# Gated attention and hash-routed experts on one core: the small token blocks of the experts, cut in halves and turned round on TensorE

## The chip, the cores and the metric

The kernel runs on one NeuronCore of one Trainium2 chip. The metric is device time in microseconds (us) of one execution; the smaller the better. A profiled execution comes with it: a span, busy times of the engines, and a trace. In the profile PE is TensorE's matrix multiplication, PEld its loading of the stationary operand, DVE is VectorE, ACT ScalarE, POOL GpSimd, and SP the engine that issues most DMAs. All data is float32. The profile writes two records for every float32 matmul, and two loads of the stationary operand.

## The reference

```python
# attention: u, v (8, 2496, 256), z (8, 2496, 64)
scores = (1 / S) * np.matmul(z, z.transpose(0, 2, 1))
attn = np.maximum(scores, 0.0) ** 2
x = (u * np.matmul(attn, v)).reshape(B * S, D)          # 19968 tokens of 256
# experts: w1 (8, 256, 1024), w2 (8, 1024, 256)
expert_idx = token_ids * np.int64(2654435761) % np.int64(8)
for e in range(8):
    xe = x[expert_idx == e]
    out[expert_idx == e] = np.maximum(xe @ w1[e], 0.0) @ w2[e]
```

Each of the 19968 tokens goes through the one expert that its id selects. With the fixed inputs of the reference, the eight experts get 2483, 2535, 2394, 2497, 2468, 2469, 2634 and 2488 tokens.

## The kernel before

**Attention.** The 2496 tokens of a batch are 20 tiles of 128 (the last has 64 rows). Queries are taken in five groups of four tiles, so there are 40 groups. For each group TensorE makes `s_ps` (scores, one matmul of up to 512 columns per key tile; the contraction is only 64 deep, and neighbouring tiles sit on the lower and the upper 64 partitions of `zT`, so that they use the two halves of the array's rows), ScalarE takes ReLU and square into `a`, and TensorE sums `acc`, which is v times `a` (L350; L358 for the 64-row tile). Scores are symmetric: VectorE transposes 32x32 blocks of `a` into tiles `m` ("mirrors") for later groups instead of computing them again (`turns_of`, L257). Some pairs of groups (`CARRIED`) are turned as a whole into `stage` (L261) and moved to their partitions by DMA, with one of the four moves a ScalarE copy (L270). How many transposes are put in at each step is planned by `turn_scores` with a budget of VectorE time, and `turn_now` puts in what is left when a tile is about to be read or its room reused. `between()` runs at each step and hands out small work: the routing arithmetic in `places()` for the first `SORT` steps, then the writing of each token's slot (`enter`), and of gated rows into `x_rows` in DRAM, in slot order (`place_x`).

**First batch.** `load_z` brings z by DMA on SP, VectorE copies one tile, TensorE transposes pairs of tiles into `z_ps` (`turn_z`), and VectorE and ScalarE copy the halves into `zT`. Six matmuls on zeros (`warm`) run before.

**Experts.** Slots are grouped by expert. 32 *wholes* have 512 tokens each (`NW`), and what remains of each expert is cut into *parts* of 128 tokens. At most 35 parts can be needed (`NP`); 33 of them (`NU`) are run always, and an `If` covers the rest, which these inputs don't need: they fill 32. The order is written out by hand: whole, part, whole, part, ..., with one part more at the end: 65 blocks.

For each block `load_x` fetches its tokens, `load_w` fetches w1 and w2 of its expert (1 MB each), `turn_x` transposes 32x32 blocks of the tokens on VectorE, `ups` multiplies by w1, and ReLU goes in turn to ScalarE and VectorE (L776, L778). `down` multiplies by w2 for 128 tokens at a time (L784); ScalarE copies the result, and GpSimd scatters the rows to `out` (L796). In `ups` w1 is the stationary operand and the tokens move:

```python
for i in range(m):                       # m = 1 in a whole, 4 in a part
    for c in range(DP):                  # DP = 2
        nc.tensor.matmul(ps[:, ts(i, n)], w1[j][:, c, ts(k * m + i, P)], xT[j][:, :, c, :], ...)
```

So a whole has 16 matmuls with 512 moving columns, a part 16 with 128. Both give `hT`, activations with features on partitions, which `down` takes as the stationary operand, while w2 moves 256 columns: 8 matmuls for each 128 tokens.

`run` is a software pipeline. In step i it issues the load of the tokens of block i + 2, then the banks of `ups` of block i with the `down`s of block i - 1 put between them (a part's `down` comes after two banks of the whole that follows; a whole's four `down`s come after the second bank of the part), then the weights of block i + 2. There are three pairs of weight buffers, which are mirrors that attention no longer needs. PSUM has six banks for `h_ps`, `s_ps`, `z_ps` (one pool, `mm_ps`) and two for `o_ps` and `acc`.

Of the kernel before, what the change touches and what calls it, by code (L numbers as in the profile page):

```python
# [24 lines left out]
def kernel(  # L25
# [33 lines left out]

    BLK = 512  # L60
    NW = -(-(N - E * (BLK - 1)) // BLK)
    NP = (N - NW * BLK + E * (P - 1)) // P
    NU = (N - NW * BLK) // P + E // 2 + 1
    NB = NW + NP
    CLEAR = T // 2
    NS = NW * BLK // P + NP
# [61 lines left out]
    def load_z(b):  # L128
        if b == 0:

            zn[b] = npool.tile([P, T + 1, K], F32, name="zn")
            tiles_io(zf, b, range(T), zn[b][:, 1:, :], False, nc.sync, twice=True)
            nc.vector.tensor_copy(zn[b][:, 0, :], zn[b][:, T, :])
            return
        zn[b] = npool.tile([P, T, NQ, Q], F32, name="zn")
        rows = zf[ds(b * S, S), :]
        for q in range(NQ):
            cols = ts(q % 2, Q)
            o = zn[b][ts(q, Q)]
            for t, m in ((slice(0, TM), rows[0:SM, cols].rearrange("(j i t) k -> i t j k", i=Q, t=TM)),  # L140
                         (TM, rows[SM:S, cols].rearrange("(j i) k -> i j k", i=Q))):
                if t == TM:
                    for h in range(2):
                        nc.sync.dma_start(o[:, TM, ds(h * R // Q, R // Q), :], m)
                else:
                    nc.sync.dma_start(o[:, t], m)
# [10 lines left out]
    def turn_z(b, g):  # L157
        if g == 0:
            zT[b] = zpool.tile([P, T * P], F32, name="zT")
        o = zT[b][:, ts(g, G * P)]  # L160
        if b:
            nc.vector.transpose(o, zn[b][:, ts(g, G)].rearrange("p t j k -> p (t j k)"))
            return


        ps = mm_ps.tile([P, G * P], F32, name="z_ps", tag="mm")
        for i, t in enumerate(group(g)):
            nc.tensor.transpose(ps[:, ts(i, P)], zn[b][:, t:t + 2].rearrange("p t k -> p (t k)"), ident[:])
        nc.vector.tensor_copy(o[K:P], ps[K:P, :])  # L169
        i = 0 if g else 1  # L170
        nc.scalar.copy(zT[b][0:K, ds((g * G + i - 1) * P, (G - i) * P)], ps[0:K, i * P:])  # L171
        return ps
# [74 lines left out]
    def turns_of(b, a, g):  # L247
# [10 lines left out]
        def carry(c):  # L258
            m = room()
            stage = spool.tile([P, G * G * Q], F32, name="stage")  # L260
            nc.vector.transpose(stage[:].rearrange("p (n q) -> p n q", q=Q), x[:, :, ts(c, Q)])  # L261
            for r in range(NQ):

                n = tiles_of(g, r)
                o = m[ts(c, Q), 0:n, r].rearrange("p i s q -> p i (s q)")
                y = stage[ts(r, Q), 0:n * G * Q].rearrange("p (i x) -> p i x", i=n)
                if r != c:
                    nc.sync.dma_start(o, y)
                else:
                    to_fetch.append((i + 3, key, lambda o=o, y=y: nc.scalar.copy(o, y)))  # L270
# [33 lines left out]
    def turn_scores(steps):  # L304
# [5 lines left out]
        carried = i % 2  # L310
# [14 lines left out]
    def fetch(due):  # L325
        for e in [e for e in to_fetch if due(e)]:
            to_fetch.remove(e)
            e[2]()

    def turn_now(key):  # L330
        for e in [e for e in to_turn if e[0] == key]:
            turn(e)
        fetch(lambda e: e[1] == key)
# [27 lines left out]
    def gate(b, g, h, acc):  # L361
# [26 lines left out]
        to_fetch.append((i + 3, None, rows_of_x))  # L388
# [15 lines left out]
    def clear_x(k):  # L404
        c = NW * BLK // P + k * -(-NP // CLEAR)
        n = min(NS - c, -(-NP // CLEAR))
# [10 lines left out]
    def places():  # L417

        with tc.tile_pool(name="route", bufs=1) as route:
# [3 lines left out]
            iota_b = route.tile([1, NP], F32)  # L423
            nc.gpsimd.iota(iota_b[:], pattern=[[1, NP]], base=0, channel_multiplier=0,
# [17 lines left out]
            mask = room[:, E * C:E * C + E * C // 2].bitcast(BF16).rearrange("p (e c) -> p e c", e=E)  # L442

# [18 lines left out]
            for e in range(0, E, H):  # L462
# [17 lines left out]
            per_e = route.tile([P, 12, E], F32)  # L480
            first, count, whole, upto_w, before_w, rest, parts, upto_p, thr, start, jump, late = (
                per_e[:, k, :] for k in range(12))
# [7 lines left out]
            int_e = route.tile([P, E], I32)  # L490
            nc.vector.tensor_copy(int_e[:], count)
# [11 lines left out]
            nc.vector.tensor_scalar(int_e[:], rest, float(P - 1), None, op0=OP.add)  # L503
            nc.vector.tensor_scalar(int_e[:], int_e[:], P.bit_length() - 1, None, op0=OP.logical_shift_right)
            yield
            nc.vector.tensor_copy(parts, int_e[:])
            nc.vector.tensor_tensor_scan(upto_p, ones[:, 0:E], parts, 0.0, op0=OP.mult, op1=OP.add)
            yield

# [7 lines left out]
            yield  # L517

            def wide(a):
                return a.unsqueeze(2).to_broadcast([P, E, C])  # L520

            nc.vector.tensor_tensor(total, rank, wide(thr), op=OP.is_ge)
            yield
            nc.gpsimd.tensor_mul(total, total, wide(jump))
            yield
# [3 lines left out]
            ahead = upto[:, :, C - G - 1]  # L529
# [7 lines left out]
            nc.gpsimd.tensor_add(rank, rank, total)  # L537
            least = route.tile([P, 1], F32)
            nc.vector.tensor_reduce(least[:], late, axis=AX.X, op=OP.min)
            yield  # L540
# [4 lines left out]
            nc.vector.tensor_copy(used[:], upto_p[0:1, E - 1:E])  # L545
# [4 lines left out]

            over = route.tile([1, NB, E], F32)
            for a, n, ends in ((0, NW, upto_w), (NW, NP, upto_p)):
                nc.vector.tensor_tensor(
                    over[:, a:a + n], ends[0:1].unsqueeze(1).to_broadcast([1, n, E]),
                    iota_b[:, 0:n].unsqueeze(2).to_broadcast([1, n, E]), op=OP.is_le)
            yield
            eb = route.tile([1, NB], F32)
            nc.vector.tensor_reduce(eb[:], over[:], axis=AX.X, op=OP.add)
            yield
            nc.vector.tensor_scalar(eb_i[:], eb[:], float(E - 1), None, op0=OP.min)  # L560
            for _ in range(5):
                yield
# [37 lines left out]
    WARM = 6  # L600
    order = tc.manual_schedule()
    order.__enter__()


# [4 lines left out]
    load_z(0)  # L609
# [3 lines left out]
    z_ps = [turn_z(0, g) for g in range(NG)]  # L613
    nc.scalar.copy(zT[0][0:K, ts(TM, P)], z_ps[0][0:K, 0:P])
# [9 lines left out]
    SORT = 2 * T + 12  # L624
# [20 lines left out]
    w1, w2, xg, xT, hT, w_buf, xg_buf, xT_buf = {}, {}, {}, {}, {}, [], [], []  # L645
# [14 lines left out]
    def load_w(j, k):  # L660
        w1[j] = w_buf[2 * k][:].rearrange("p i r s q -> p (i r s q)").rearrange("p (h f) -> p h f", h=DP)
        w2[j] = w_buf[2 * k + 1][:].rearrange("p i r s q -> p (i r s q)").rearrange("p (c d) -> p c d", c=FP)
        e = nc.sync.value_load(eb_i[0:1, j:j + 1], min_val=0, max_val=E - 1)
        for r in range(NQ):
            rows = moe_w1[ds(e, 1), ts(r, D // NQ)].rearrange("one d f -> (one d) f")
            nc.sync.dma_start(w1[j][ts(r, Q), :, :], rows.rearrange("(h i) f -> i h f", i=Q))
        nc.sync.dma_start(
            w2[j], moe_w2[ds(e, 1)].rearrange("one f d -> (one f) d").rearrange("(c p) d -> p c d", p=P))
# [4 lines left out]
    def turn_x(j, k):  # L673
        xT[j] = xT_buf[k][:, 0:slots(j)[1] * P // Q]
        nc.vector.transpose(xT[j].rearrange("p k h i -> p (k h i)"), xg[j].rearrange("p k d -> p (k d)"))
# [6 lines left out]
    for n, (b, g) in enumerate(groups):  # L682
# [12 lines left out]
        for t in range(EARLY, TM - LATE):  # L695
            if g == NG - 1 and b + 1 < B and t % 2 == 0 and t // 2 > 2:
                turn_z(b + 1, t // 2 - 3)
            if n + 1 == len(groups) and t == T // 4:

                w_buf = list(mirrors)  # L700
                w_buf.extend(mirror[b, a, g] for a in range(NG - 1))
                load_w(0, 0)
# [51 lines left out]
    nc.gpsimd.memset(o_all[:, 0:BLK // P * AHEAD + NP - NU, :], 0.0)  # L754
    xT_buf.append(turned_x(o_all, T // XW - 1))

# [4 lines left out]

    def ups(j):

        n = slots(j)[1] * P
        m = BLK // n
        tiles = [apool.tile([P, G, BLK], F32, name="hT", tag="a") for _ in range(-(-FP // (G * m)))]
        hT[j] = [tiles[f // (G * m)][:, f // m % G, ds(f % m * n, n)] for f in range(FP)]
        for k in range(FP // m):
            ps = mm_ps.tile([P, BLK], F32, name="h_ps", tag="mm")
            for i in range(m):  # L770
                for c in range(DP):
                    nc.tensor.matmul(ps[:, ts(i, n)], w1[j][:, c, ts(k * m + i, P)], xT[j][:, :, c, :],  # L772
                                     start=(c == 0), stop=(c == DP - 1))
            o = tiles[k // G][:, k % G, :]
            if k % 2 == 0:
                nc.scalar.activation(o, ps[:], AF.Relu)  # L776
            else:
                nc.vector.tensor_scalar_max(o, ps[:], 0.0)  # L778
            yield

    def down(j, t, later):
        ps = acc_ps.tile([P, D], F32, name="o_ps", tag="acc")
        for f in range(FP):
            nc.tensor.matmul(ps[:], hT[j][f][:, ts(t, P)], w2[j][:, f, :], start=(f == 0), stop=(f == FP - 1))  # L784
# [17 lines left out]
    def run(work, first, last, loads, later=None):  # L802

        for i in range(first, last + 1):
# [8 lines left out]
            up = ups(work[i]) if i < last else None  # L813
            for k in banks:
# [3 lines left out]
                if k % 2 == 1:  # L818
                    for _ in range(-(-len(do) * 2 // (len(banks) - k + 1))):
                        do.pop(0)()  # L820
            for f in do:
                f()
            if i < last and i + 2 < loads:
                load_w(work[i + 2], (i + 2) % LOADS)
# [4 lines left out]

    assert NU == NW + 1 and NP <= NW + NU  # L830
    work = [j + k for j in range(NW) for k in (0, NW)] + [NW + NU - 1]
    NM = len(work) - 3
    load_w(work[1], 1)
# [7 lines left out]
    with tc.If(n_used > NU):  # L841
        for j in [*range(AHEAD), *range(NW + NU, NB)]:
            load_x(j, (NM + 2) % LOADS)
            load_w(j, (NM + 2) % LOADS)
# [35 lines left out]
```

## Time and profile before

| what | value |
|---|---|
| median of 3 runs | 2635.14 us (2635.05 to 2635.41) |
| the profiled execution's own time | 2636.14 us |
| its span in the trace | 2634.3 us |
| PE busy in the span | 2627.5 us |
| DVE, ACT, POOL busy | 1230.1, 647.3, 605.4 us |
| first scores, first `acc` matmul | 8.99 us, 18.13 us |
| first matmul of the experts | 1514.89 us |
| mean DMA rate | 120 GB/s |

The span is shorter than the profiled execution's time by 1.84 us, which lie around it. That execution is 1.0 us above the median. A row of the profile gives a source line, an engine, an operation, output and inputs, shapes and a count, then busy time and the mean duration of one. Matmuls are pipelined, so that the mean of one is longer than the distance from one to the next: the pace is read from the start times in the timeline.

### The profile page before, as it was taken

The numbers are of one execution on the slowest core, as the hardware profiler recorded it, in microseconds if no ns is written. First come the engines' busy times: TensorE is split into PE (matmuls) and PEld (weight loads), VectorE is DVE, ScalarE is ACT, GpSimd is POOL, SyncE is SP. The second block draws the span as 40 slices with busy tenths as digits, with TensorE's granted clock in tenths as the row PEclk, the third lists the DMA queues.
The fourth block names the chain that finished last, engine by engine and source line by source line (L and its number), as shares of the span: only waits on it lengthen the run. The fifth ranks groups of instructions, "written<-read, shape, count | busy, mean of one in ns | idle before, by whom it ended". The sixth has DMA issues, their size and how long they took to land.

```text
span 2634.3 us, 27069 instructions
## 1 busy us (share of the span) xinstructions
PE 2627.5 (100%) x8854; PEld 1527.0 (58%) x8854; DVE 1230.1 (47%) x2775; ACT 647.3 (25%) x1368; POOL 605.4 (23%) x667
## 2 busy tenths in 40 slices
PE   9999999999999999999999999999999999999999
PEld 5444444444444444444444477777777777777777
DVE  6777768766866776758767611111111111111111
ACT  6215323333234134143153011111111111111111
POOL 1332233133242332233212221111111111111112
PEclk9999999999999999999999999999999999999999
DMA  3443333332423423423422386766666666666663
GB/s 119 124 111 77 79 96 92 79 100 72 114 74 71 112 77 83 114 58 102 106 55 76 103 203 166 165 166 158 158 156 155 157 155 153 165 166 164 167 158 84
DMA packets 432080, 315.43 MB, mean 120 GB/s; under 512 B 266908, under 2 KB 394925, under 8 KB 431936
## 3 DMA queue, kind: packets, MB, share of 16 engines
q1 hardware_dynamic: 410192, 272.27, 42.8%
q0 software_dynamic: 20736, 41.09, 4.9%
q8 instruction: 72, 1.18, 0.2%
q14 instruction: 72, 0.59, 0.1%
q10 hardware_dynamic: 1008, 0.30, 0.1%
HBM read 229.36 MB, written 67.53 MB: 113 GB/s over the span
## 4 chain that ended last, share of the span: by engine, by line
PE 57%; issue 35%; POOL 6%; POOLq 0%; DMA 0%; DVE 0%; ACT 0%; ACTq 0%; DVEq 0%
PE acc L350 49%; PE s_ps L219 7%; POOL out_dram L796 6%; PE acc L358 2%; POOLq L796 0%; PE warm L608 0%; DMA x_sb<-x_way 0%; DMA x_way<-x_q 0%; POOL x_rows L594 0%; DVE hT L778 0%; POOL v_sb L754 0%; DVE x_sb L386 0%; DVE zT L169 0%; POOLq L875 0%; POOLq L839 0%
## 5 line engine op out<-in xcount | busy, mean ns | idle before, releaser
L350 PE MATMUL acc<-a,v_sb 128*128 128x512 f32 (+1 forms) x1760 | 765.9, 592 | 0.0
L257 DVE STREAM_TRANSPOSE m<-a 32x512 f32<-32x512 f32 (+1 forms) x896 | 604.0, 674 | 20.2 <-ACT a L235 5.2
L772 PE MATMUL h_ps<-v_sb,m 128*128 128x128 f32 (+1 forms) x2080 | 567.9, 431 | 0.9 <-ACTq L841 0.9
L350 PEld LDWEIGHTS acc<-a,v_sb 128*128 128x128 f32 x1760 | 342.2, 196 | 390.5 <-issue 373.1
L784 PE MATMUL o_ps<-m,hT 128*128 128x256 f32 x2576 | 566.3, 379 | 0.0
L778 DVE TENSOR_SCALAR hT<-h_ps 128x512 f32<-128x512 f32 x161 | 111.2, 691 | 928.6 <-PE h_ps L772 928.6
L784 PEld LDWEIGHTS o_ps<-m,hT 128*128 128x128 f32 x2576 | 487.0, 190 | 78.1 <-issue 14.8
L350 PE MATMUL acc<-m,v_sb 128*128 128x512 f32 (+1 forms) x1280 | 527.5, 571 | 0.0
L772 PEld LDWEIGHTS h_ps<-v_sb,m 128*128 128x128 f32 x2080 | 317.5, 191 | 235.0 <-issue 230.4
L350 PEld LDWEIGHTS acc<-m,v_sb 128*128 128x128 f32 x1280 | 251.1, 196 | 272.1 <-issue 267.7
L796 POOL DMA_INDIRECT out_dram<-o_sb,idx x157 | 153.5, 977 | 921.7 <-ACT o_sb L791 913.8
L227 ACT ACTIVATE a<-s_ps 128x512 f32<-128x512 f32 (+3 forms) x456 | 202.0, 584 | 567.8 <-PE s_ps L219 479.1
L386 POOL TENSOR_TENSOR x_sb<-x_sb,u_sb 128x256 f32<-128x256 f32 (+1 forms) x156 | 108.2, 721 | 926.8 <-DMA x_sb<-x_way 926.8
L286 DVE STREAM_TRANSPOSE a<-a 32x128 f32<-32x128 f32 (+2 forms) x1360 | 281.3, 239 | 9.6
L235 ACT ACTIVATE a<-a 128x512 f32<-128x512 f32 (+1 forms) x480 | 227.9, 568 | 0.6
L791 ACT COPY o_sb<-o_ps 128x256 f32<-128x256 f32 x161 | 59.9, 372 | 595.1 <-PE o_ps L784 595.1
L366 DVE STREAM_TRANSPOSE x_q<-acc 128x512 f32<-128x512 f32 (+1 forms) x80 | 56.4, 706 | 296.0 <-PE acc L350 283.5
L776 ACT ACTIVATE hT<-h_ps 128x512 f32<-128x512 f32 x161 | 96.0, 597 | 397.0 <-PE h_ps L772 387.6
L219 PE MATMUL s_ps<-zT 64*128 64x512 f32 (+1 forms) x960 | 188.7, 536 | 0.3 <-ACT zT L171 0.3
L594 POOL DMA_INDIRECT x_rows<-x_sb,slot_i x160 | 157.6, 985 | 64.1 <-issue 36.6
L582 POOL DMA_INDIRECT slot_tokens<-token,addr x160 | 156.2, 976 | 48.6 <-issue 48.6
L219 PEld LDWEIGHTS s_ps<-zT 64*128 64x128 f32 x960 | 112.4, 186 | 93.5 <-issue 63.3
(95 smaller groups left out, 353.3 us busy)
## 6 DMA issues: line engine op xcount, KB each, us to landing
m<-in_moe_w_dram SPq DMA_DIRECT2D x260, 256.0 KB
m<-in_moe_w_dram SPq DMA_DIRECT2D x65, 1024.0 KB
v_sb<-in_v_dram SPq DMA_DIRECT2D x32, 512.0 KB
u_sb<-in_u_dram SPq DMA_DIRECT2D x32, 512.0 KB
x_way<-x_q SPq DMA_DIRECT2D x128, 128.0 KB
x_sb<-x_way SPq DMA_DIRECT2D x32, 512.0 KB
v_sb<-x_rows SPq DMA_DIRECT2D x128, 128.0 KB
m<-stage SPq DMA_DIRECT2D x240, 64.0 KB
```

The source lines that it names most:

```text
L219: nc.tensor.matmul(ps[:, lo:n], zT[b][h, ts(t, P)], zT[b][h, ds(g * G * P + lo, n - lo)], start=True, stop=True)
L227: nc.scalar.activation(a, ps[:, lo:n], AF.Relu)
L235: nc.scalar.activation(a, a, AF.Square, scale=1.0 / S)
L257: nc.vector.transpose(o, x[ts(r, Q), 0:m * G, ts(c, Q)].rearrange("p (i s) q -> p i s q", s=G))
L286: return n * Q, lambda: nc.vector.transpose(out, in_)
L350: nc.tensor.matmul(acc[h][:, 0:queries(g)], v_sb[b][:, t, h::2], squares(b, g, t), start=(k == 0), stop=(k == TM - 1), skip_group_check=True)
L582: st = nc.gpsimd.indirect_dma_start(out=slot_dram[:, None], out_offset=bass.IndirectOffsetOnAxis(ap=addr[0:n, c:c + 1], axis=0), in_=token ...
L594: st = nc.gpsimd.indirect_dma_start(out=x_dram[:, :], out_offset=bass.IndirectOffsetOnAxis(ap=slot_i[0:width(c % T), c:c + 1], axis=0), in ...
L772: nc.tensor.matmul(ps[:, ts(i, n)], w1[j][:, c, ts(k * m + i, P)], xT[j][:, :, c, :], start=(c == 0), stop=(c == DP - 1))
L778: nc.vector.tensor_scalar_max(o, ps[:], 0.0)
L784: nc.tensor.matmul(ps[:], hT[j][f][:, ts(t, P)], w2[j][:, f, :], start=(f == 0), stop=(f == FP - 1))
L796: st = nc.gpsimd.indirect_dma_start(out=out[:], out_offset=bass.IndirectOffsetOnAxis(ap=rows, axis=0), in_=o, in_offset=None, bounds_check ...
```

## The change

*Halves.* The rest of an expert is now cut into parts of 128 and at most one half of 64. 27 parts are run always, and the halves go two at a time: a *pair* is a block of 128 slots whose lower 64 belong to one expert and whose upper 64 to another (or to the same, if an expert's 28th part stands there). Four pairs are run always. The order is whole, part or pair, ..., whole: 32 wholes, 27 parts, 4 pairs, 63 blocks. These inputs fill 28 parts and 4 halves, which is 60 of the 62 half blocks at hand, so that the `If` is not entered.

*Tokens stand still.* In parts and pairs (`ups_of_part`) the tokens are the stationary operand and w1 moves 512 columns. The activations come out with tokens on partitions, and VectorE turns them with 16 transposes of 32 partitions by 256 elements. In a pair the two halves use their own 64 columns of the array (tile size 128 by 64 in the instruction), their own weights, and the partitions 0 to 63 and 64 to 127 of one PSUM bank; their matmuls alternate. The same holds in `down`.

*Order.* The `down` of a part or a pair comes after all banks of the whole that follows (`late`). A fourth pair of weight buffers is made from the tiles of `zn` and `zT`; buffers are taken from a queue, and a pair takes two.

*Attention.* z of the first batch is loaded on the queues of SP and ScalarE, without the copy on VectorE; one transpose group more; the copies of the two halves of `zT` are declared independent; three warm-up matmuls instead of six. Carried turns go by DMA alone (no ScalarE copy), and one is put in at every third step instead of every second. `places()` has the arithmetic for halves, and `SORT` grows by 6.

```diff
-    NP = (N - NW * BLK + E * (P - 1)) // P
-    NU = (N - NW * BLK) // P + E // 2 + 1
+    HALF = P // 2
+    NP = (N - NW * BLK) // P - 1
+    NH = E
+    MH = max(NH, (N - NW * BLK + E * (HALF - 1)) // HALF - 2 * NP)
...
 def load_z(b):
-            tiles_io(zf, b, range(T), zn[b][:, 1:, :], False, nc.sync, twice=True)
-            nc.vector.tensor_copy(zn[b][:, 0, :], zn[b][:, T, :])
+            for tiles, eng in ((range(2 * G), nc.sync), (range(2 * G, TM), nc.scalar), ([TM], nc.sync)):
+                tiles_io(zf, b, tiles, zn[b][:, tiles[0] + 1:, :], False, eng, twice=True)
...
 def carry(c):
-                if r != c:
-                    nc.sync.dma_start(o, y)
-                else:
-                    to_fetch.append((i + 3, key, lambda o=o, y=y: nc.scalar.copy(o, y)))
+                nc.sync.dma_start(o, y)
...
 def turn_scores(steps):
-        carried = i % 2
+        carried = i % 3
...
-    SORT = 2 * T + 12
+    SORT = 2 * T + 18
...
+    def halves(j, h, n=P):
+        return ts(h, n // 2) if len(w1[j]) > 1 else slice(0, n)
...
+    def ups_of_part(j):
+        tile = apool.tile([P, G, BLK], F32, name="hT", tag="a")
+        rows = tile[:, 0:G // 2, :].rearrange("p k (f x) -> p (k f) x", x=P)
+        turned = tile[:, G // 2:G, :].rearrange("p k (f x) -> p (k f) x", x=P)
+        hT[j] = [turned[:, f, :] for f in range(FP)]
+        for k in range(F // BLK):
+            ps = mm_ps.tile([P, BLK], F32, name="h_ps", tag="mm")
+            for c in range(DP):
+                for h, w in enumerate(w1[j]):
+                    x = xT[j][:, halves(j, h, NQ), c, :].rearrange("p k i -> p (k i)")
+                    nc.tensor.matmul(ps[halves(j, h), :], x, w[:, c, ts(k, BLK)], start=(c == 0), stop=(c == DP - 1),
+                                     skip_group_check=True)
+            relu(k, tile[:, k, :], ps)
+            yield
+        for r in range(NQ):
+            for c in range(NQ):
+                nc.vector.transpose(turned[ts(c, Q), :, ts(r, Q)], rows[ts(r, Q), :, ts(c, Q)])
...
 def down(j, t, later):
         for f in range(FP):
-            nc.tensor.matmul(ps[:], hT[j][f][:, ts(t, P)], w2[j][:, f, :], start=(f == 0), stop=(f == FP - 1))
+            for h, w in enumerate(w2[j]):
+                cols = halves(j, h)
+                nc.tensor.matmul(ps[cols, :], hT[j][f][:, ts(t, P)][:, cols], w[:, f, :],
+                                 start=(f == 0), stop=(f == FP - 1), skip_group_check=True)
...
 def run(work, first, last, loads, later=None):
-            up = ups(work[i]) if i < last else None
+            up = (ups_of_part if work[i] >= NW else ups)(work[i]) if i < last else None
+            late = i > first and work[i - 1] >= NW
             for k in banks:
                 next(up)
...
-                if k % 2 == 1:
+                if k % 2 == 1 and not late:
...
+            if i > first:
+                w_free.extend(sets.pop(work[i - 1]))
             if i < last and i + 2 < loads:
-                load_w(work[i + 2], (i + 2) % LOADS)
+                load_w(work[i + 2])
...
-    work = [j + k for j in range(NW) for k in (0, NW)] + [NW + NU - 1]
+    NU = NP + NH // 2
+    small = [*range(NW, NW + NP)]
+    for k in range(NH // 2):
+        small.insert((k + 1) * NU // (NH // 2 + 1), NW + NP + k)
+    work = [j for pair in zip(range(NW - 1), small) for j in pair] + [NW - 1]
```

## The prediction

> **What bounds the kernel now.** I read the engines' shares first, then the list of what PE waited for, then the rows of PE by form, and last the timeline for the pace of each block.
>
> ```profile
> PE 2627.5 (100%) x8854; PEld 1527.0 (58%) x8854; DVE 1230.1 (47%) x2775; ACT 647.3 (25%) x1368; POOL 605.4 (23%) x667
> DVE  6777768766866776758767611111111111111111
> PEclk9999999999999999999999999999999999999999
> DMA  3443333332423423423422386766666666666663
> ...
> PE warm L608 <- POOL zero L96: 1.2, 1, 1.2
> PE h_ps L772 <- ACTq L841: 0.9, 1, 0.9
> PE s_ps L219 <- ACT zT L171: 0.3, 1, 0.3
> ```
>
> PE is busy all the time at the full granted clock, and after the start it waits 0.9 us in all. So only fewer or faster matmuls, or an earlier start, can shorten the time; and each wait that the change brings in costs its full length. In the experts (right half of the slices) VectorE is a tenth busy, DMA two thirds.
>
> The timeline of PE gives the price of each block. A busy time counts overlapped ends, so I take the distance from start to start.
>
> ```profile
> 1514.89 13.90 PE L772 MATMUL h_ps<-v_sb,m 128*128 128x512 f32 x32
> 1528.62 13.98 PE L784 MATMUL o_ps<-m,hT 128*128 128x256 f32 x64
> 1542.44 7.38 PE L772 MATMUL h_ps<-v_sb,m 128*128 128x128 f32 x40
> 1549.66 3.62 PE L784 MATMUL o_ps<-m,hT 128*128 128x256 f32 x16
> 1553.12 14.03 PE L772 MATMUL h_ps<-v_sb,m 128*128 128x512 f32 x56
> ...
> 2619.16 3.73 PE L772 MATMUL h_ps<-v_sb,m 128*128 128x128 f32 x32
> 2622.74 7.07 PE L784 MATMUL o_ps<-m,hT 128*128 128x256 f32 x32
> ```
>
> A whole's `ups` take 1528.62 - 1514.89 = 13.73 us for 32 records, 0.429 each of 512 columns. Its four `down`s take 13.82 for 64 records, 0.216 each of 256. A part's `ups` take 2622.74 - 2619.16 = 3.58 (32 records, 0.112 each of 128), its `down` 3.46. A whole and a part together recur every 34.57 us (the chain of waits steps from 1900.71 to 1935.29), which gives 3.56 for the part's `ups`; I use 3.57. PE's cost is columns moved, with a few ns per record.
>
> **Parts.** 33 parts cost 33 x (3.57 + 3.46) = 232.0 us. With the tokens standing still a part's `ups` are 4 matmuls of 512 columns, 8 records x 0.429 = 3.43; `down` is as before. 27 x (3.43 + 3.46) = 186.0. The turn of operands by itself is worth 0.14 per part.
>
> **Pairs.** A pair moves two weight matrices: 8 matmuls of 512 columns (16 records, 6.87 us one after the other), then 16 of 256 (32 records, 6.91), so 13.78 if its halves take turns. It is worth doing only if the two column halves of the array work at once. No row of before shows column halves. The nearest rows are the row halves of attention, where two matmuls stand on 64 rows each:
>
> ```profile
> 48.02 6.64 PE s_ps L219 x32
> 54.66 32.82 PE acc L350 x76
> ...
> 85.60 1.88 PE L350 MATMUL acc<-a,v_sb 128*128 128x512 f32 x4
> 87.41 1.14 PE L358 MATMUL acc<-a,v_sb 64*128 64x512 f32 x4
> 88.38 1.88 PE L219 MATMUL s_ps<-zT 64*128 64x512 f32 x8
> ```
>
> The 16 score matmuls from 48.02 (14 of 512 columns, 2 of 256) would take 7680 x 13.73/8192 = 12.87 us in turn; they took 6.64, a ratio of 0.52. The two records of one matmul go one after the other on their half, the second beside the first of the other half; so n records take (n + 1)/2 steps. The four records of L358, with a full-array matmul ahead and row halves after, took 0.97: entering that mode has no visible price. By this a pair's `ups` are 17/2 x 0.429 = 3.65 and its `down` 33/2 x 0.216 = 3.56, with 0.1 for eight changes of mode: 7.3. Four: 29.2.
> The Trainium skill speaks of columns directly. "TensorE: Matmul & The Clock Gate", section "Measured speedup vs the span model", has three column tiles of 32 at 2.38 times, 79% of the ideal. By that a pair is 13.78/(2 x 0.79) = 8.7, four are 34.9, an estimate. I take the row of this trace, whose data are float32 with the same alternation, and keep the page for the range: 5.7 us.
> The same page, "The mechanism", speaks against the change: loads of the stationary operand overlap running matmuls only if the row group differs. Column halves have the same rows. By its rate for a load (columns over 1.2 GHz, "LDWEIGHTS") 64 columns are 53 ns, and 4 x 48 loads laid bare would be 10.2 us, an estimate. But in this trace the loads of L784 (2510 of 190 ns) stand in the same row group as the matmuls beside them, which keep 0.216 us apart; the measurement decides, and I take nothing. I keep 10.2 for a rival.
>
> Parts and pairs: 232.0 - 186.0 - 29.2 = 16.8 us gained.
>
> **What the moved `down` waits for.** A part's `down` now waits for 16 transposes of 32x256. VectorE's 32x128 takes 302 ns and 32x384 takes 570 (rows of L286 and L257), so about 436 each, 7.0 in all; behind the last ReLU (0.69) and the whole's `turn_x` (1.24) they end 9 us after the part's `ups`. The cover is four `down`s (13.82) and eight banks (13.73). Without it each of 31 would bare up to 9 us. Queued behind on VectorE is the next whole's ReLU of bank 1, which can't start before 13.82 + 3.43. Only at the first part is there no `down` in between: that ReLU comes some 5.5 us late, but bank 7 is the first that needs its PSUM room (six banks), and 12 us have gone by then. Nothing for either. In the experts VectorE goes from 5.0 to 12.0 of 34.6 us.
>
> **Weights.** A part's buffers come free 10.3 us later than before, behind the whole's banks. But with four sets and three in use, an ordinary block takes the set of i - 2, free at the start of step i, so SP can issue earlier than now. A pair's second set is free after the whole's `down`s and due 17.2 us later, for 2 MB. In a step of two blocks DMA is busy 0.66 x 34.6 = 22.8 us for 5.5 MB; 2 MB more make 8.3 us, 31.1 of 34.6. It fits; cost nothing. Laid bare whole it would be 4 x 8.3 = 33. SP's queue behind such a wait is the next `load_x`, due two blocks later.
>
> **Start.** Scores begin at 8.99, and `acc` at 18.13.
>
> ```profile
> 1.18 5.37 PE L608 MATMUL warm<-zero 128*128 128x256 f32 x12 [1.18 <-POOL zero L96]
> 5.45 0.20 DVE L133 COPY zn<-zn 128x64 f32<-128x64 f32 x1 [5.45 <-DMA zn<-in_z_dram]
> 7.75 3.01 ACT L171 COPY zT<-z_ps 64x384 f32<-64x384 f32 x5 [5.45 <-DVE zT L169]
> 8.99 9.20 PE L219 MATMUL s_ps<-zT 64*128 64x512 f32 x40 [0.26 <-ACT zT L171]
> ```
>
> z is there at 5.45; ScalarE's copies then wait for VectorE's (7.03 to 7.65). Without the VectorE copies ahead, and with z in two queues, I expect transposes from about 4.3, ScalarE's second copy at 6.9 and scores from 7.1: 1.8 us, which stay, since PE does not wait later. Bounds: 2.8 gained if z lands a us earlier still; 1 lost, because only six warm-up records run and these are at half pace (5.37/12 = 0.45 for 256 columns), so scores may begin at that pace. I take 1.8.
>
> **The rest of attention.** 96 ScalarE copies (57 us of ScalarE, which has slack) become DMAs of up to 64 KB on SP. With one carried turn in three steps more of them are still open when `turn_now` wants their room: following the planner's list, two in each of seven batches before, 29 in all after, at most three at once. Each is 707 ns of VectorE just ahead of scores. Before, two at 232.5 ended 1.7 us ahead of the first ReLU, and PE never waited; one more fits. Routing adds some 3.5 us to VectorE (a 1494 ns compare and a dozen of 0.17) and 5.2 to POOL (2324 and 2913 ns), where VectorE is 77% busy and PE waits for neither. All these: nothing to 15 x 0.71 + 3.5 = 14 if nothing covered them; I take 0.5, by the empty list of waits. A gain is excluded: PE has no wait there to lose. After the last matmul nothing changes.
>
> **Sum.** 16.8 + 1.8 - 0.5 = 18.1. Span 2634.3 - 18.1 = 2616.2; with the 1.84 around it 2618.0; the profiled execution stands 1.0 above the median, so 2617.0. About 0.2% (5.3 us) is what a measurement can tell from no change: 2629.9 to 2640.4.
>
> **Rivals.**
> 1. *Column halves at once, with a toll* (the page's 79%, bare loads, or drains): 2622.6 by the first, 2627.2 by the second. For: no row shows columns. Against: row halves have no toll. 20%.
> 2. *Slower: the halves take turns*, in `ups_of_part` and `down` of the four pairs. Then four cost 55.1 instead of 29.2, and 2617.0 + 25.9 = 2642.9. It turns at a pair of (232.0 + 1.3 - 186.0)/4 = 11.8 us, a ratio of 0.86. For: both halves read all 128 partitions of moving data, twice what a row pair reads, and four bytes an element; against: the page's three tiles. 14%.
> 3. *PE waits*: a pair's weights come late, or forced transposes delay scores. Half of one bound, 7 us of attention or 17 of DMA, gives 2624 to 2634. For: DMA would be 90% busy there. Against: idle slices between transfers now. 6%.
> 4. The change might not do what it says by entering the `If`: 28 full parts and 4 halves are 60, the limit 62. Left out.
>
> Forecast: 60%, with a range of its own from 2612 to 2622. To leave out no more than 2 in 10 the range goes up to 2632, which takes in most of rivals 1 and 3. Faster by over 0.2%: 0.60 and most of rivals 1 and 3, 0.80; the same 0.06; slower 0.14.
>
> **What would show it.** In the timeline a pair's `ups` near 3.7 us from start to start and its `down` near 3.6 (6.9 each would be rival 2); a part's `ups` 3.43; no new row in PE's list of waits; first scores near 7.1, first `acc` near 16.3, experts from 1513.6. The forecast is wrong if pairs exceed 8 us, or if the experts begin later than 1515.

## The result, and the profile after

The changed kernel takes 2619.01 us (median of 6 runs, 2618.62 to 2619.56); the kernel before, on the same chip, 2635.3 (6 runs). The ratio is 0.9938, with a 95% interval of 0.9927 to 0.9948: 16.3 us less. A second measurement gave 2618.53 against 2635.26, ratio 0.9937 (0.9924 to 0.9951): 16.7 us less. The forecast was 18.1 us less, 2617.0.

One correction first. The token counts given ahead of the prediction, and the "28 parts and 4 halves, 60 of 62" there and in rival 4, are wrong: they are not those of the reference's fixed inputs. The right counts are 2506, 2446, 2582, 2478, 2498, 2473, 2434 and 2551. They fill all 33 parts of the kernel before, and 28 parts and 5 halves of the changed one: 61 of 62 half blocks. The `If` is entered in neither, as was said, but with one half block to spare and not two. It matters in one experiment below.

The page of the changed kernel, engines and slices:

```profile
PE 2610.0 (100%) x8105; PEld 1441.9 (55%) x8105; DVE 1453.5 (56%) x3285; ACT 584.2 (22%) x1268; POOL 607.4 (23%) x668
DVE  7977768767766866767758633333333333333332
```

What its PE waited for, in all, how often, longest:

```profile
PE warm L652 <- POOL zero L102: 1.2, 1, 1.2
PE h_ps L834 <- PEq L938: 0.7, 1, 0.7
PE z_ps L176 <- DMA zn<-in_z_dram: 0.5, 1, 0.5
```

PE is the bound as before; VectorE has gone from one to three tenths in the experts, and nothing waits for it. PE's busy time fell by 17.5 us. The timeline of PE shows where. Each line is a run of matmuls: start, length with overlapped ends, shape, records. The shape 128*64 is a matmul on half of the array's columns.

```profile
1513.52 13.90 PE L834 MATMUL h_ps<-v_sb,m 128*128 128x512 f32 x32
...
1541.06 3.60 PE L855 MATMUL h_ps<-m,v_sb 128*128 128x512 f32 x8
1544.50 13.90 PE L834 MATMUL h_ps<-v_sb,m 128*128 128x512 f32 x32
...
1716.66 13.90 PE L834 MATMUL h_ps<-v_sb,m 128*128 128x512 f32 x32
1730.40 3.62 PE L869 MATMUL o_ps<-zT,hT 128*128 128x256 f32 x16
1733.94 3.65 PE L855 MATMUL h_ps<-m,v_sb 128*64 128x512 f32 x16
1737.53 14.08 PE L869 MATMUL o_ps<-m,hT 128*128 128x256 f32 x64
1751.44 13.90 PE L834 MATMUL h_ps<-v_sb,zn 128*128 128x512 f32 x32
1765.27 3.67 PE L869 MATMUL o_ps<-m,hT 128*64 128x256 f32 x32
1768.88 3.70 PE L855 MATMUL h_ps<-m,v_sb 128*128 128x512 f32 x8
...
1786.23 13.90 PE L834 MATMUL h_ps<-v_sb,m 128*128 128x512 f32 x32
...
1820.66 9.60 PE L834 MATMUL h_ps<-v_sb,zn 128*128 128x512 f32 x22
```

A part's `ups` take 3.44 us (1541.06 to 1544.50). An ordinary step of two blocks takes 1820.66 - 1786.23 = 34.43; the step with the pair's `ups` 1751.44 - 1716.66 = 34.78, the one with its `down` 34.79. So a pair costs 6.89 + 0.35 + 0.36 = 7.6 us for work that is 13.78 in turn. At its start, matmul by matmul:

```profile
1941.24 0.64 PE L855 MATMUL h_ps<-m,v_sb 128*64 128x512 f32 x1
1941.24 0.64 PE L855 MATMUL h_ps<-zn,v_sb 128*64 128x512 f32 x1
1941.72 0.59 PE L855 MATMUL h_ps<-m,v_sb 128*64 128x512 f32 x1
1941.72 0.59 PE L855 MATMUL h_ps<-zn,v_sb 128*64 128x512 f32 x1
...
1944.29 0.59 PE L855 MATMUL h_ps<-m,v_sb 128*64 128x512 f32 x1
1944.82 1.35 PE L869 MATMUL o_ps<-m,hT 128*128 128x256 f32 x5
```

`m` and `zn` hold the weights of the two halves. Both start within 0.01 us of each other, again and again: the halves run at once. The first step is longer, 0.48 instead of 0.43, and so is the last, 0.53 up to the full-width matmul that follows.

### The profile page after: what moved, and what is told of

The parts are those of the page before. It is cut to its first block, busy times and chain, and to the rows that moved or that the text cites. A ratio compares the mean times of both kernels' runs of the same rounds, so it can differ in the third digit from the quotient of the medians.

```text
span 2617.4 us, 26062 instructions
## 1 busy us (share of the span) xinstructions
PE 2610.0 (100%) x8105; PEld 1441.9 (55%) x8105; DVE 1453.5 (56%) x3285; ACT 584.2 (22%) x1268; POOL 607.4 (23%) x668
## 4 chain that ended last, share of the span: by engine, by line
PE 58%; issue 35%; POOL 6%; DMA 0%; POOLq 0%; DVE 0%; ACTq 0%; DVEq 0%
PE acc L359 49%; PE s_ps L232 7%; POOL out_dram L882 6%; PE acc L367 2%; POOLq L882 0%; PE z_ps L176 0%; DMA zn<-in_z_dram 0%; DMA x_way<-x_q 0%; DMA x_sb<-x_way 0%; POOL x_rows L637 0%; DVE hT L842 0%; DVE x_sb L395 0%; POOLq L972 0%; POOLq L936 0%; POOL v_sb L811 0%
## 5 line engine op out<-in xcount | busy, mean ns | idle before, releaser
L869 PE MATMUL o_ps<-m,hT 128*128 128x256 f32 (+1 forms) x2064 | 446.9, 379 | 0.0
L869 PEld LDWEIGHTS o_ps<-m,hT 128*128 128x128 f32 (+1 forms) x2064 | 382.3, 188 | 75.9 <-issue 24.3
L834 PE MATMUL h_ps<-v_sb,m 128*128 128x512 f32 x832 | 361.4, 592 | 0.7 <-PEq L938 0.7
L834 PEld LDWEIGHTS h_ps<-v_sb,m 128*128 128x128 f32 x832 | 158.0, 190 | 189.7 <-issue 188.5
L861 DVE STREAM_TRANSPOSE hT<-hT 32x256 f32<-32x256 f32 x496 | 214.9, 433 | 6.5
```

Of the source, the lines that this page charges most:

```text
L834: nc.tensor.matmul(ps[:], w1[j][0][:, c, ts(f, P)], xT[j][:, :, c, :], start=(c == 0), stop=(c == DP - 1))
L861: nc.vector.transpose(turned[ts(c, Q), :, ts(r, Q)], rows[ts(r, Q), :, ts(c, Q)])
L869: nc.tensor.matmul(ps[cols, :], hT[j][f][:, ts(t, P)][:, cols], w[:, f, :], start=(f == 0), stop=(f == FP - 1), skip_group_check=True)
```

## Experiments

**1. Does TensorE need neighbours on different halves?**

```diff
-            for c in range(DP):
-                for h, w in enumerate(w1[j]):
+            for h, w in enumerate(w1[j]):
+                for c in range(DP):
...
-        for f in range(FP):
-            for h, w in enumerate(w2[j]):
+        for h, w in enumerate(w2[j]):
+            for f in range(FP):
```

> The changed kernel, but in a pair all matmuls of the lower half come ahead of those of the upper half (loops over half and contraction swapped in ups, over half and feature block in down). Nothing else moves. Theory: two matmuls run at once only where neighbours in the queue stand on different column halves. Then only the neighbours at each border overlap, a pair takes 12 to 13.8 us instead of about 7.6, and four pairs make it 17 to 25 us slower: 2636 to 2644 us. Rival: TensorE reaches past queued matmuls of the same half, or the halves were never what saved the time: 2619 us, no change.

Measured: 2629.53 us (10 runs; before 2635.78), 10.5 us slower than the changed kernel. Neither held. Its timeline of PE at the first pair and, finer, in the `down` of a later one:

```profile
1733.09 3.70 PE L855 MATMUL h_ps<-m,v_sb 128*64 128x512 f32 x16
1736.73 14.08 PE L869 MATMUL o_ps<-m,hT 128*128 128x256 f32 x64
...
1764.47 6.31 PE L869 MATMUL o_ps<-m,hT 128*64 128x256 f32 x32
1770.71 3.70 PE L855 MATMUL h_ps<-m,v_sb 128*128 128x512 f32 x8
...
2184.44 3.02 PE L869 MATMUL o_ps<-zT,hT 128*64 128x256 f32 x13
2187.09 0.43 PE L869 MATMUL o_ps<-m,hT 128*64 128x256 f32 x1
2187.30 0.38 PE L869 MATMUL o_ps<-zT,hT 128*64 128x256 f32 x1
```

`ups` still take 3.64 us although four records of one half now stand in a row (two matmuls, two records each). `down`, with 16 in a row, takes 6.24 instead of 3.61: four times 2.63 is the 10.5 us. There the upper half's first record (`m`) starts beside the lower half's 13th, when three lower ones still wait: 12 steps of the lower half alone, then 16 of the upper, 28 in all. Both readings fit one rule: a record starts as soon as its half is free and no more than three records ahead of it in the order have not started. "TensorE: Matmul & The Clock Gate" of the Trainium skill, section "Step-by-step: what each phase is for", says that matmuls stay in program order and only loads are pulled ahead. In this trace matmuls of the other half pass up to three that wait; the measurement decides.

**2. Is the reach three?** A rule made from one run has to foretell another. Runs of eight:

```diff
-            for c in range(DP):
-                for h, w in enumerate(w1[j]):
...
+                    for h, w in enumerate(w1[j]):
+                        for q in range(2):
+                            for c in range(DP):
...
-        for f in range(FP):
-            for h, w in enumerate(w2[j]):
+        for f, h, w in [(f, h, w) for q in range(2) for h, w in enumerate(w2[j]) for f in range(q * G, q * G + G)]:
```

> The changed kernel, with a pair's matmuls in runs of eight records of one half (ups: both banks of the lower half, then both of the upper; down: four feature blocks of the lower half, four of the upper, and again). Theory: TensorE reaches past three waiting records. Then ups take 12 steps of 0.429 instead of 8 (5.3 us from start to start), down 21 of 0.216 instead of 16 (4.7), and four pairs make it 11 us slower: 2630 us. Rivals: a reach of two gives 13 and 24 steps (5.7 and 5.3 us, 15 us slower), of four 11 and 19 (4.9 and 4.3, 8 us slower); a run of four passes by another cause and a run of eight by none: 16 and 31 steps, 26 us slower.

Measured: 2630.34 us (14 runs), 11.8 us slower than the changed kernel in the same comparison (2618.53). The timeline of PE at the first pair:

```profile
1734.00 5.42 PE L860 MATMUL h_ps<-m,v_sb 128*64 128x512 f32 x16
1739.35 14.08 PE L880 MATMUL o_ps<-m,hT 128*128 128x256 f32 x64
...
1767.09 4.70 PE L880 MATMUL o_ps<-m,hT 128*64 128x256 f32 x32
1771.72 3.70 PE L867 MATMUL h_ps<-m,v_sb 128*128 128x512 f32 x8
```

The `ups` take 5.35 us, the 12 steps of the expectation; a reach of two would have been 5.7, of four 4.9. The `down` shows the rule record by record, here in the second pair (`m` is the lower half, `zT` the upper):

```profile
1977.18 1.29 PE L880 MATMUL o_ps<-m,hT 128*64 128x256 f32 x5
1978.10 0.43 PE L880 MATMUL o_ps<-zT,hT 128*64 128x256 f32 x1
...
1978.80 0.59 PE L880 MATMUL o_ps<-zT,hT 128*64 128x256 f32 x2
1979.02 0.43 PE L880 MATMUL o_ps<-m,hT 128*64 128x256 f32 x1
```

The upper half's first record starts beside the lower's fifth, the lower's ninth beside the upper's fifth, the upper's ninth, at 1979.94, beside the lower's 13th. Each time exactly three records ahead of it still wait. By the rule this makes 20 steps, 4.32 us; the expectation's 21 was one too many. The rest of the 4.63 is 0.05 at each of the four starts of a half and 0.1 at the end. The order of a pair's matmuls thus sets its time, and the order of the change, alternating one by one, is within the reach.

**3. The turn of the operands by itself.** The kernel before with `ups_of_part` for its parts and the later `down`:

```diff
-            up = ups(work[i]) if i < last else None
+            up = (ups_of_part if work[i] >= NW else ups)(work[i]) if i < last else None
+            late = i > first and work[i - 1] >= NW
...
-                if k % 2 == 1:
+                if k % 2 == 1 and not late:
```

> The kernel before with one part of the change: in whole parts the tokens stand still, w1 moves, VectorE turns the activations, and their down comes after the banks of the whole that follows. No halves, 33 parts, 65 blocks, three sets of weights, the old start. Theory: the turn of the operands alone is worth 0.14 us a part, 33 x 0.14 = 4.6 us: 2630.7 us, and the other 11 us of the gain are the two blocks that the pairs save. Rival: most of the gain comes from the operands or from the order, and it goes to 2624 us or below. Second rival: with three sets of weights the later release of a part's set makes TensorE wait, and it is no faster than 2635 us.

Measured: 2638.1 us (12 runs), ratio 1.0011 (1.0002 to 1.002): slower than before. The timeline of PE and VectorE shows why, at the very end, where two parts stand next to each other:

```profile
2616.71 3.62 PE L807 MATMUL o_ps<-m,hT 128*128 128x256 f32 x16
2617.71 7.18 DVE L802 STREAM_TRANSPOSE hT<-hT 32x256 f32<-32x256 f32 x16
2624.99 5.81 PE L807 MATMUL o_ps<-m,hT 128*128 128x256 f32 x16 [4.66 <-issue]
```

The last part's `down` needs the 16 transposes, and the only cover is one `down` of 3.46 us. The row gives the release as "issue", but the transposes end at 2624.89 and the matmuls start at 2624.99. After the wait the 16 records take 5.81 and not 3.62. So 4.7 of wait and 2.2 of slow matmuls: 6.9 us. (The clock granted to TensorE was half of full speed, 0.50, from 2622.5 to 2629.2; experiment 4 tells of it.) To see that nothing else was lost, the last block was given its w1-stationary `ups` again:

```diff
-            up = (ups_of_part if work[i] >= NW else ups)(work[i]) if i < last else None
+            up = (ups_of_part if NW <= work[i] < NW + NU - 1 else ups)(work[i]) if i < last else None
```

> The kernel of the parts-only run, but the last block, a part that follows a part directly, has w1 stationary again, so that no transposes stand between its ups and its down. Theory: the parts-only run lost 4.7 us of wait and about 2.2 us of slow matmuls after it at that one place; without it the turn of the operands brings 32 x 0.14 = 4.5 us, and the time is 2631 us. Rival: with three sets of weights and the later down something else is lost too, and it stays at 2634 us or above.

Measured: 2631.98 us (20 runs; before 2635.53), ratio 0.9986 (0.998 to 0.9993), 3.6 us faster than before, with a wide spread (2630.59 to 2633.04). No wait is left in PE's list but the kernel before's own. From the first matmul of the experts to the end of the span it takes 2628.8 - 1513.63 = 1115.2 us against 1119.4, 4.2 less for 32 parts, and up to the start of the last `down` 4.7 less, where the theory has 4.5. The median is 1 us off the theory; the profile is that of the fastest of the 20 runs.

The other way round, w1 stationary again in the 27 parts of the changed kernel:

```diff
+            if len(w1[j]) == 1:
+                for q in range(BLK // P):
+                    for c in range(DP):
+                        nc.tensor.matmul(ps[:, ts(q, P)], w1[j][0][:, c, ts(k * (BLK // P) + q, P)], xT[j][:, :, c, :], ...)
...
+        if len(w1[j]) == 1:
+            hT[j] = [rows[:, f, :] for f in range(FP)]
+            return
```

> The changed kernel, with w1 stationary again in the 27 whole parts (16 matmuls with 128 moving columns, no transposes of activations); pairs, order and start stay. Theory: 27 x 0.14 = 3.8 us slower: 2622.8 us, with a part's ups at 3.57 us again. Rival: the 16 transposes a part on VectorE cost about what the operands save, and it stays within 1 us of 2619.

Measured: 2624.4 us (4 runs; before 2635.78), 5.4 us slower than the first 2619.0. A part's `ups` in its timeline:

```profile
1632.50 3.73 PE L855 MATMUL h_ps<-v_sb,zn 128*128 128x128 f32 x32
1636.08 13.98 PE L880 MATMUL o_ps<-m,hT 128*128 128x256 f32 x64
```

3.58 us again. The experts take 2622.5 - 1515.05 = 1107.5 us, 3.6 more than the changed kernel's 2617.4 - 1513.52 = 1103.9. So the operands are worth about the 0.14 a part that was forecast, 0.13 here; the rest of the 5.4 does not lie in the experts. In this profile they began 1.5 us later, of which experiment 5 tells, and the kernel before, measured beside it, was 0.5 us slower than beside the 2619.0.

**4. What covers the transposes.**

```diff
-            late = i > first and work[i - 1] >= NW
+            late = False
```

> The changed kernel, but a part's or pair's down comes after two banks of the whole that follows, as before, not after all eight. Theory: the transposes end 9 us after the part's ups, and four downs and two banks (17.3 us) cover that; only the first part has no downs ahead, so its down waits 5 to 6 us once: 2624.5 us. Rival: the late order is what hides the transposes, each of 31 blocks waits several us, and it is more than 20 us slower.

Measured: 2625.56 us (5 runs), 6.5 us slower than 2619.0. PE waits once, at the first part, and at none of the other 30. The timeline there:

```profile
1545.20 7.18 DVE L861 STREAM_TRANSPOSE hT<-hT 32x256 f32<-32x256 f32 x16
1552.48 5.38 PE L869 MATMUL o_ps<-m,hT 128*128 128x256 f32 x16 [4.68 <-issue]
```

Busy times of PE in three stretches of the same run; the number after the count in brackets is the clock granted to TensorE, as a share of full speed:

```profile
1549.00:1553.00 4.00, 0.52 (x3) 1.00 1.05 261
1553.10:1556.40 3.30, 3.30 (x10) 0.50 1.36 223
1556.60:1560.00 3.40, 3.40 (x12) 1.00 1.05 227
```

The later `down` is needed at the first part alone. The wait itself is 4.68 us. Just after it the clock is half for 3.41 us (1553.08 to 1556.49 in the trace's clock record), and 16 records take 5.21 us (1552.48 to 1557.69) where they take 3.46 elsewhere. 4.68 + 1.75 = 6.4, about the measured difference. The Trainium skill, "TensorE: Matmul & The Clock Gate", section "What's actually happening", has the clock fall to half after an idle window of some 3.4 us. The half agrees, and so does the length: in these traces the time from one change of the clock to the next is a whole multiple of 3.41 us (one here, two in the first run of experiment 3, 764 in the first profile of the changed kernel). But a window need not be idle throughout. Of those at full clock that a wait fell into, the ones with 2.10 us or more without work were followed by half the clock (2.82 here, 2.13 in the first run of experiment 3, 2.10 in experiment 6), and the ones with 1.87 (here) or 0.90 (the kernel before, ahead of its `If`) were not.

**5. The start and the rest of attention.** All of that undone in the changed kernel, the experts kept:

```diff
-            for tiles, eng in ((range(2 * G), nc.sync), (range(2 * G, TM), nc.scalar), ([TM], nc.sync)):
-                tiles_io(zf, b, tiles, zn[b][:, tiles[0] + 1:, :], False, eng, twice=True)
+            tiles_io(zf, b, range(T), zn[b][:, 1:, :], False, nc.sync, twice=True)
+            nc.vector.tensor_copy(zn[b][:, 0, :], zn[b][:, T, :])
...
-        carried = i % 3
+        carried = i % 2
...
-    WARM = 3
+    WARM = 6
```

> The changed kernel with the parts of attention undone: z on one queue with the copy on VectorE, six warm-up matmuls, dependent copies of zT, carried turns as before (ScalarE copy, every second step). Theory: those parts bring about 1 us at the start and nothing after it, so it is 0.5 to 1.3 us slower than the changed kernel: about 2619.6 us if that is at 2618.8. Rival: the carries cost or bring something over eight batches as well, and it differs by 2 us or more either way.

Measured: 2619.97 us (5 runs, 2619.45 to 2620.3), against 2618.53 and 2619.01 of the changed kernel: 1.0 to 1.4 us slower. The start of the changed kernel:

```profile
4.63 3.68 PE L176 MATMUL z_ps<-ident,zn 128*128 128x128 f32 x21 [0.52 <-DMA zn<-in_z_dram]
8.24 8.85 PE L232 MATMUL s_ps<-zT 64*128 64x512 f32 x40
17.02 19.16 PE L359 MATMUL acc<-a,v_sb 128*128 128x512 f32 x44
```

z lands at 4.6, near the 4.3 of the forecast, but the 21 transposes take 3.6 us where 20 took 2.35 before, and scores follow them: 8.24 and not 7.1. Would one more warm-up matmul mend it? The changed kernel was run again beside it:

> The changed kernel once more, beside the others of this job. 2619 us; first scores between 7.3 and 9.7 us after the span's start, as in the profiles so far, which had the same start in three of five kernels and differed by 2.3 us.

> The changed kernel with four warm-up matmuls instead of three (8 records at half pace, to 4.6 us, where z lands). Theory: the transposes of z run at half pace because too little work stands ahead of them; then 21 of them take under 3 us and scores begin at 7.4 us: 0.5 us faster than the changed kernel. Rival: the time at which z lands, and the moment at which the pace turns, vary by themselves: no difference that can be told, within 0.4 us.

Measured: 2618.53 and 2618.71 us, five runs each: no difference, as the rival said. Seven profiles with this same start have the 21 transposes in 2.48 to 4.71 us, first scores from 7.04 to 9.61, and the first `acc` from 15.85 to 18.55: a single profile says little about a microsecond here. The traces show what varies: the moment at which TensorE's clock rises. Their clock record begins with the rise to full speed, at 7.10 us in the profile above, at 4.41 in the changed kernel's second one, at 9.97 in that of w1 stationary again (experiment 3). In the profile above the transposes follow each other every 0.213 us up to the rise and every 0.109 after it. In the other two all 21 lie on one side of it:

```profile
4.63 2.48 PE L176 MATMUL z_ps<-ident,zn 128*128 128x128 f32 x21 [0.52 <-DMA zn<-in_z_dram]
4.96 4.71 PE L176 MATMUL z_ps<-ident,zn 128*128 128x128 f32 x21 [0.85 <-DMA zn<-in_z_dram]
```

In the four profiles with the old start the six warm-up matmuls last beyond the rise (4.19 to 6.30 us), and the transposes take 2.35 to 2.38 each time. There the warm-up's own length, 4.33 to 5.37 us, moved the rest (`acc` at 17.13 to 18.13): VectorE's copy of z was done 0.1 to 0.7 us before the transposes began. From the first `acc` to the experts it is 1496.76 us before, 1496.50 after and 1496.49 with attention undone, so the carries cost and bring nothing.

**6. One pair less.** An attempt at a faster version, and at a pair's price:

```diff
-    NH = E
+    NH = E - 2
...
-    work = [j for pair in zip(range(NW - 1), small) for j in pair] + [NW - 1]
+    work = [j for pair in zip(range(NW - 2), small) for j in pair] + [NW - 2, NW - 1]
```

> The changed kernel with three pairs always run instead of four (60 half blocks, which these inputs just fill; the If covers the rest as before): 62 blocks, the last two both wholes. Theory: a pair costs 7.6 us on TensorE wherever it stands, and nothing waits: 7.6 us faster, 2611.4 us if the changed kernel is at 2619.0. Rival: a part ahead of two wholes in a row, or the weights of two wholes in a row, make TensorE wait, and less than 4 us is left.

Measured: 2676.25 us (5 runs), 57.7 us slower. Here the wrong count told: 61 half blocks are in use and 60 at hand, so the `If` ran. The timeline of PE there:

```profile
2541.25 13.90 PE L834 MATMUL h_ps<-v_sb,m 128*128 128x512 f32 x32
...
2599.05 6.03 PE L869 MATMUL o_ps<-m,hT 128*128 128x256 f32 x16 [8.12 <-DVE hT L861]
2604.91 3.60 PE L855 MATMUL h_ps<-m,v_sb 128*128 128x512 f32 x8
2610.61 15.66 PE L834 MATMUL h_ps<-v_sb,zn 128*128 128x512 f32 x32 [2.10 <-issue]
```

From 2541.25 to 2604.91 stands a whole, a pair and a part one after the other, 63.7 us with waits for transposes. Take off the pair that is saved, 7.6, and add the wait of 2.1 us after it and 1.8 for the whole behind that wait, which runs partly at half the clock (15.50 us instead of 13.73). That makes 60.0; the profiled execution, 2677.82 us, was 59.3 above the 2618.53. What a pair is worth by leaving it out was therefore not measured; its price of 7.6 us rests on the timeline. With 27 parts, four pairs are the fewest for these inputs.

No version beat the changed kernel.

## Why the prediction was right, step by step

*What bounds it*: PE, in both kernels, with no wait of the change's own. Right.

*Parts*: 0.14 each from the turn of the operands, 3.8 in all. Right: 3.6 and 4.2 us in the experts' part of two traces (experiment 3).

*Pairs*: 7.3 forecast, 7.6 measured; the direction and nearly all of the size right, two of its parts wrong, and both come from one reading of the rows of before. The steps were counted as (n + 1)/2, the second record of a matmul beside the first of the next; in fact both halves start together, and it is n/2 (16 records in 8 steps). And "entering that mode has no visible price", "0.1 for eight changes of mode", is the mis-sized term: each stretch of column halves costs 0.35 us beyond its steps: 0.1 in the step before it, 0.05 in its first, 0.1 in its last, 0.1 in the one after it. Four pairs have eight stretches. 8 x 0.35 = 2.8 us. The first error gave back 4 x 0.32 = 1.3, so that four pairs cost 30.4 and not 29.2: it is luck that the two errors partly cancel. The price could be read in the trace of before. There the row halves start in pairs too:

```profile
86.89 0.59 PE L350 MATMUL acc<-a,v_sb 128*128 128x512 f32 x1
87.41 0.71 PE L358 MATMUL acc<-a,v_sb 64*128 64x512 f32 x2
```

The step ahead of them is 0.52 us instead of 0.43, and the 0.97 of the four L358 records are two steps of 0.43 and 0.11 besides. The half step in (n + 1)/2 was part of the price under another name. What the price is made of, no run shows.

*The Trainium skill's two rules* (page "TensorE: Matmul & The Clock Gate"): by the first, in "Measured speedup vs the span model", a pair was estimated at 8.7 us, at 79% of the ideal; measured are 13.78/7.6 = 1.8 times, 91%, tolls and all. By the second, in "The mechanism", loads overlap running matmuls only where row groups differ. That is not so here: the 64-column loads, 0.13 to 0.14 us each, share the rows with the matmuls beside them, and the steps stay at 0.43 and 0.216.

*The later `down`*: transposes of 436 ns forecast, 433 measured (the row is below), and the cover as stated, with the one weak place at the first part, named in the forecast and shown by experiment 4. Experiment 3 found a second such place in another order of blocks.

```profile
L861 DVE STREAM_TRANSPOSE hT<-hT 32x256 f32<-32x256 f32 x496 | 214.9, 433 | 6.5
```

*Weights*: forecast at nothing, and PE never waits for them, in steps with pairs too. DMA was busy 0.82 of the fuller of the first pair's two steps, where 0.90 was reckoned.

*Start*: 1.8 forecast, 1.0 to 1.4 measured with the whole of attention undone. z came 0.3 us later than said; what was taken at nothing was TensorE's half clock, at which 12 of the 21 transposes still ran in the first profile, and which the text had as a bound ("1 lost"). How late the clock rises differs from execution to execution, so this term could not have been forecast to better than about a microsecond.

*The rest of attention*: 0.5 kept back, nothing used.

*After the last matmul*: "nothing changes" is open by 0.5 us. The changed kernel's span ends 5.2 us after the last matmuls should (their start and 80 x 0.216), that of before 4.65. But the run of experiment 5 with the old start has 5.2 as well, and the second parts-only run, which ends with the same blocks as the kernel before, 5.1; so it may be the one profile of before that stands apart. This is not settled.

*Sum*: pairs 1.2 less, start 0.6 less in the mean, the end 0.5 less if that is real, against 0.5 held back and not needed: 18.1 becomes 16.3, which is what the first comparison gave. That it fits to the tenth is luck; the second gave 16.7.

*Rivals*: the toll of rival 1 is there, but four pairs cost 1.2 us more than forecast, where it had 5.7 or 10.2. (Its 2622.6 should be 2622.7, and its 10.2 took the page's 53 ns for a load, where the trace of before had 190 ns for 128 columns; inside a stretch no load lay bare.) Rival 2, halves in turn, is nearly what experiment 1 made of `down`: 6.24 us of 6.91. Rival 3 did not come.

## What to carry to other kernels

Blocks that fill only half of TensorE's columns can be run two at a time with two sets of weights, at nearly twice the pace, if their matmuls alternate in the order or at least change sides every four records (four in a row cost nothing, eight did). Keep such stretches few, as each cost a third of a microsecond. Where an operand's layout has to be turned on another engine between two matmuls of one chain, look for the one place in the order that has no other work ahead of it: one such place cost more than the operands saved in 33 blocks. And price a wait of TensorE at more than its length where half the clock can follow: 4.7 us of wait cost 6.4 to 6.9, 2.1 us cost 3.9, and 0.9 us nothing more.

## What the runs showed of the hardware

Matmuls on the other column half pass up to three records that wait for their own half (experiments 1 and 2: 28, 12 and 20 steps, and the records one by one). A float32 matmul's two records are no unit in this: each half goes on by itself. Going into and out of column halves cost 0.35 us a stretch.

TensorE's granted clock was full or half, and changed at whole multiples of 3.41 us. A stretch of that length with 2.10 us or more of waiting was followed by half the clock, one with 1.87 us was not. With half the clock for 3.41 us, 1.8 us were lost in experiments 4 and 6. At the start the clock rose at 4.2 to 10.0 us after the span's beginning, in kernels whose first steps are nearly the same, and with z's landing this moved the first `acc` by up to 2.7 us.
